# Margins in a planner that writes out the order of work: five constants of a fused attention and GLU kernel

## The chip, the cores and the metric

The kernel runs on one core of one Trainium2 chip. The metric is the device time of one execution in microseconds (us), lower is better. Before the change five runs took 881.21, 882.92, 887.68, 879.78 and 884.89 us; the median is 882.92 us. The run with 881.21 us is the one whose profile is read here.

The core has five engines, each with an instruction queue of its own that it works off in order: TensorE (PE, matrix products into PSUM), ScalarE (ACT, here exp), VectorE (DVE), GpSimd (POOL) and SyncE (SP, which here issues all transfers). An instruction that waits holds up everything behind it on its engine.

## The reference

The input has 2048 rows of width 640, all in bf16. One block of attention (32 heads of width 20) and one of a bilinear GLU (width 1728) follow each other, each on a normalised copy of its input:

```python
qkv = (x @ wqkv).reshape(B, S, 3, H, Dh) ...
scores = jnp.einsum("bhqd,bhkd->bhqk", q, k) * (Dh ** -0.5)
p = _softmax(scores, axis=-1)
o = jnp.einsum("bhqk,bhkd->bhqd", p, v)
...
h = x + _A_ref(_layernorm(x, axis=-1), A_wqkv, A_wo)
h2 = h + _B_ref(_layernorm(h, axis=-1), B_w_gate, B_w_up, B_w_down)
```

`_B_ref` is `((x @ w_gate) * (x @ w_up)) @ w_down`. The exp of the scores is the largest piece outside the products: 32 heads of 2048 by 2048.

## The kernel before

**Tiling.** The queries are cut into five chunks (`CHUNKS`, L37: three of 512 columns, two of 256), the heads into eight groups of four. A unit of attention is one PSUM bank: scores of 128 keys against 512 queries of one head (or two key tiles against 256 queries), transposed, so that keys lie on partitions. There are 2048 units. Four heads run side by side in the rows of TensorE for the scores (L1008), and side by side in its columns for the product with V (L1159), which adds up in the one bank ACC. V carries a column of ones, so that the sums of the softmax come out of the same product.

**Two ways for exp.** ACT takes three banks at once (SA into a buffer EA) or two (SB into EB), L1083. DVE takes a unit from one of the banks D0 and D1: L1108 turns a score into the bits of a bf16 exponential with one multiply and add, into a buffer Y. L1118 makes two shifted copies of it, and L1116 a third on POOL; the sum of the four is the approximation of exp. TensorE adds them up, so a unit of DVE brings four products with V where a unit of ACT brings one.

**Background jobs.** Everything else on TensorE is a list of jobs: the projections to Q, K and V, the output projection (WO), and for each half of a chunk (256 rows) the gate and up products (14 jobs) and the down products (4 jobs). A job takes a bank (D0 or D1 while attention runs, any bank after it), issues its products (L1334 in the column mode, L1311 over the full array) and is read by DVE: L329 copies, L842 multiplies gate by up into HH, L766 and L869 add the residual. When the last group of a half has its softmax sums, a layer normalisation follows (L433 to L458, and a transposing transfer L<-t, L474), then the gate and up jobs.

**The order is planned in Python.** The kernel does not loop over tiles. A list scheduler runs while the kernel is built: it has a clock `now[0]`, gives each operation a length by a formula (`c_act`, `c_psum`, `c_fast`, `c_pool`, L67 to L80), lets each engine take the ready operation with the lowest key, and writes instructions down in the order in which its clock starts them. Only the order is kept. On the chip, semaphores make every instruction wait for what it needs, in that order. If the plan expects a result too early, the instruction stands at the head of its queue and blocks the others; if it expects it too late, other work goes first.

**What the plan expects of results.**
- `LAT` (L60, 0.12): from the end of an operation on ACT, DVE or POOL to its reader on another engine.
- `LATP` (L61, 0.23): from the end of a product, as planned (0.216 for 512 columns), to its reader. It is used where a job's bank is read (`job_done`, L1280), where ACT reads a set (L1085), where DVE reads a D bank (L1094), where a buffer that a product has read comes free (L1161) and where ACC is read (L1176).
- `dma` (L352): a transfer takes `dur` on SP's queue and lands `lat` later, 1.25 unless stated.

**The end of a group** (`close_group`, L1173). When a group of heads has all its products, DVE copies ACC to `acs` (L1188). A transfer puts the row of sums into HBM (`dscr<-acs`, d1), a second fetches it spread over the partitions (`dn<-dscr`, d2, L1191), DVE takes the reciprocals (`rn`, L1192, with the most urgent key of DVE, -2), a third transfer writes them back, a fourth broadcasts them (`bc<-rscr`), POOL multiplies (L1217), and further transfers put the result into ON for the output projection. There are 40 such groups.

**What TensorE does next** (`pe_turn`, L1410). First, if a set SA or SB is free and the next unit's Q and K are there (`stream_ready`, L978), it refills that set (`refill`, L1032); with it go those D banks that `d_banks` (L1508) grants, whose units DVE then takes (`take_for_dve`). So a unit goes to DVE only if a D bank is free at the moment of a refill. Otherwise up to four rounds are filled with background jobs whose inputs are there (`job_ready`, L1231) and with products with V whose exp is there (`counts`, L1340). [...]

Of the kernel before, what the change touches and what calls it, by code (L numbers as in the profile page):

```python
# [57 lines left out]


LAT = 0.12  # L60
LATP = 0.23  # L61
DMA_LAT = 1.5
SWITCH = 0.105
WINDOW = 3.413
# [2 lines left out]
def c_act(n):  # L67
    return 0.10 + 0.833e-3 * n


def c_psum(n):
    return 0.075 + 1.04e-3 * n
# [73 lines left out]
def kernel(  # L146
# [21 lines left out]
    dscr = [dram.tile([1, 2048], F32, name=f"dscr{i}") for i in range(NDS)]  # L168
# [18 lines left out]
    DN = [sb.tile([P, 16], F32, name=f"dn{i}") for i in range(NDS)]  # L187
# [40 lines left out]
    now = [0.0]  # L228
    lockt = {"DVE": 0.0, "POOL": 0.0}

    def tick(t):
        heapq.heappush(wake, t)
# [7 lines left out]
    def finish(op, t, e=None, end=None):  # L240

        op.done = t
        for u in op.users:
            u.left -= 1
            u.avail = max(u.avail, end if e is not None and isinstance(u, Op) and u.engs == (e,) and e != "SP" else t)
            if u.left == 0:
                if isinstance(u, Op):
                    enqueue(u)
                else:
                    release_later(u.avail, u.cb)  # L250
        op.users = []
        tick(t)

    def add(engs, dur, fn, key, deps=(), **kw):
        if isinstance(engs, str):
            engs = (engs,)
        op = Op(engs, dur, fn, flat(key), deps, **kw)
        if op.left == 0:
            op.avail = max(op.avail, now[0])
            enqueue(op)  # L260
        return op
# [3 lines left out]
    def release_later(t, f):  # L265
        seq[0] += 1
        heapq.heappush(later, (t, seq[0], f))
        tick(t)

    def after(deps, cb):  # L270
        c = Call()
        c.left = 0
        c.avail = now[0]
        c.cb = cb
        for d in deps:
            if d.done is None:
                d.users.append(c)
                c.left += 1
            else:
                c.avail = max(c.avail, d.done)  # L280
        if c.left == 0:
            release_later(c.avail, cb)
# [48 lines left out]
    attn = {"started": False, "over": False}  # L331
# [20 lines left out]
    def dma(o, i, key, deps=(), dur=0.6, lat=1.25, kb=0):  # L352

        def hook(t, end, e):
            landed[0] = max(landed[0], end + 0.3) + kb / 330.0
            op.lat = max(lat, landed[0] - end + 1.1)
        op = add("SP", dur, lambda e: nc.sync.dma_start(o, i), key, deps, lat=lat, hook=hook)
        return op

    with tc.manual_schedule():  # L360
# [325 lines left out]
        for ci in range(len(CHUNKS)):  # L686
            q0, cw = CHUNKS[ci]
            b, off = q0 // 512, q0 % 512
# [289 lines left out]
        def stream_ready(i):  # L978
            if i >= len(stream):
                return False  # L980
            ci, g, j, kts = stream[i]
            t = now[0] + 1e-9
            for m in qj[ci, g]:
                if m.done is None or m.done > t:
                    return False
            for kt in kts:
                for m in kj[g, kt // 4]:
                    if m.done is None or m.done > t:
                        return False
            return True  # L990
# [41 lines left out]
        def refill(name, dbanks):  # L1032
# [51 lines left out]
            z = Mark()  # L1084
            z.done = end + LATP  # L1085
            act_q[name] = c_act(512 * n)
            add("ACT", c_act(512 * n), fn, (1,), [z], hook=hook, gate=lambda: bool(st["efree"]))

        def fill_d(i, it, end):
            bank = banks["D"][i]  # L1090
            bank_use["D"][i] = "exp"
            z = Mark()
            z.done = end + LATP
            ys = [None] * 4  # L1094
# [54 lines left out]
        def emit_piece(j):  # L1149
# [10 lines left out]
                             start=(n == 0), stop=last, tile_position=(0, 32 * j), skip_group_check=True)  # L1160
            release_later(end + LATP, rel)  # L1161
            if last:
# [10 lines left out]
        def close_group(ci, g, end):  # L1173
            q0, cw = CHUNKS[ci]
            z = Mark()
            z.done = end + LATP  # L1176
            k = ngrp[0] % 2
            d = ngrp[0] % NDS
            ngrp[0] += 1
            a = ACS[k]  # L1180
            acc_ready[0] = 1e9
            cg_i[0] += 1

            def hook(t, en, e):
                acc_ready[0] = en + LAT
                tick(en + LAT)
            deps = [z] + ([acs_use[k]] if acs_use[k] is not None else [])
            ev = add("DVE", c_psum(cw), lambda e: nc.vector.tensor_copy(a[:, 0:cw], ACC[:, 0:cw]), (-2,), deps, hook=hook)  # L1188
            n = cw // 32
            d1 = dma(dscr[d][0, 0:4 * cw].rearrange("(a q) -> a q", a=4), a[Dh:P:32, 0:cw], 10, [ev] + ([ds_use[d]] if ds_use[d] is not None else []), kb=8)  # L1190
            d2 = dma(DN[d][:, 0:n], dscr[d][0, 0:4 * cw].rearrange("(b c) -> b c", c=n), 10, [d1], dur=0.33, kb=8)  # L1191
            rc = add("DVE", 0.07 + 0.0064 * n, lambda e: nc.vector.reciprocal(RN[d][:, 0:n], DN[d][:, 0:n]), (-2,), [d2])  # L1192
            d3 = dma(rscr[d][0, 0:4 * cw].rearrange("(b c) -> b c", c=n), RN[d][:, 0:n], 10, [rc], dur=0.33, kb=8)
            ds_use[d] = d3
            bdeps = [d3] + ([bc_use[0]] if bc_use[0] is not None else [])
            src = rscr[d][0:1, 0:4 * cw]
            bsrc = bass.AP(tensor=src.tensor, offset=src.offset, ap=[[cw, 4], [0, 32], [1, cw]])
            d4 = [dma(BC[0][:, 0:cw], bsrc, 10, bdeps, lat=1.8 + cw / 200.0)]

            parts = []  # L1200
            for j in range(4):
                f = 20 * (4 * g + j)
                m = min(Dh, P - f % P)
                parts.append((32 * j, f, m))
                if m < Dh:
                    parts.append((32 * j + m, f + m, Dh - m))
            need = [c for c in range(KT) if any(f // P == c for _, f, _ in parts)]

            def room():
                return sum((ci, c) not in on_of for c in need) <= len(on_free) and lt_ops[NT - 1].done is not None  # L1210

            def mhook(t, en, e):
                for c in need:
                    if (ci, c) not in on_of:
                        on_of[ci, c] = on_free.pop(0)
            o = OS[k]
            mu = add("POOL", 0.1 + 2.3e-3 * cw, lambda e: nc.gpsimd.tensor_tensor(  # L1217
                o[:, 0:cw], a[:, 0:cw], BC[0][:, 0:cw], ALU.mult), (0,), d4 + os_use[k], lock=True, hook=mhook, gate=room)

            def out_of(p0, f, m):  # L1220
                return add("SP", 0.75, lambda e: nc.sync.dma_start(ON[f % P:f % P + m, on_of[ci, f // P], 0:cw], o[p0:p0 + m, 0:cw]),
                           (10,), [mu], lat=DMA_LAT)
            os_use[k] = [out_of(*p_) for p_ in parts]
            after(os_use[k], lambda: finish(mu_mark[ci, g], now[0]))
            acs_use[k] = mu
            bc_use[0] = mu
# [4 lines left out]
        def job_ready(jb):  # L1231
            if jb.can is not None and not jb.can():
                return False
            if jb.target > spos[0] + SLACK and attn["started"] and not attn["over"] and recent(now[0]) > BUSY:
                return False
            for d in jb.deps:
                if d.done is None or d.done > now[0] + 1e-9:
                    return False
            return True

# [36 lines left out]
        def job_done(jb):  # L1277
            cur_job[0] = None
            z = Mark()
            z.done = jb.end + LATP  # L1280
            op = jb.evac(banks[jb.bank[0]][jb.bank[1]], z)
# [58 lines left out]
        def counts():  # L1340
            if cg_i[0] >= len(order_cg) or acc_ready[0] > now[0] + 1e-9:
                return None
            ci, g = order_cg[cg_i[0]]
            out_ = []
            for j in range(4):
                n = 0
                for pc in pieces_q.get((ci, g, j), ()):
                    if pc[2] > now[0] + 1e-9:
                        break
                    m = vj[g // 2, pc[0]].out  # L1350
                    if m.done is None or m.done > now[0] + 1e-9:
                        break
                    n += 1
                out_.append(n)
            return out_
# [68 lines left out]
            return keep_busy()  # L1424

        BUSY = 0.55
        SLACK = 1000

        def keep_busy():

            t = now[0]
            if t < T0 or spos[0] >= len(stream) and not jq and cur_job[0] is None:
                return False
            if recent(t) > (BUSY if attn["started"] else BUSY0):
                tick(t + 0.25)
# [20 lines left out]
        ROUND = 0.216  # L1456
        SCORE = 0.216 + LATP
        MARGIN = 0.05
# [46 lines left out]
        def bg_wanted():  # L1505
            return cur_job[0] is not None or any(job_ready(jq[k]) for k in range(min(LOOK, len(jq))))
# [99 lines left out]
```

The softmax here doesn't subtract the row's maximum and nothing guards it: scores larger than these inputs give would overflow.

## Time and profile before

| | value |
|---|---|
| median of five runs | 882.92 us |
| the profiled execution, by its run's time | 881.21 us |
| its span, first to last instruction | 879.4 us |
| mean granted clock of TensorE | 0.986 |
| ACT, instructions on exp (EA, EB) | 323 and 319 |
| DVE, units of exp (L1108) | 445 |
| POOL, busy | 332.9 us (38%) |

The span falls into three parts: some 24 us of loads, normalisation and first projections, the attention from 24 us to 815 us, with background jobs in between, and 64 us after it in which the last two halves of the GLU are done. The profile's lists name an engine and a line; `EA<-SA` is an instruction that writes tile EA from SA. "Idle before" is the time an engine stood still ahead of an instruction, with the engine whose result ended the wait. Dividing groups into instructions: 323 instructions of three banks and 319 of two make about 1603 units on ACT, with some of fewer banks among them, and 445 are left for DVE.

### The profile page before, as it was taken

The page shows a single profiled execution, that of the slowest core. Times are in us where ns is not written, and L with a number is a line of the kernel's source. Part 1 is how long each engine was busy: PE and PEld are TensorE (multiplying, and loading weights), DVE is VectorE, ACT ScalarE, POOL GpSimd, SP SyncE. Part 2 cuts the span into 40 slices and gives each one's busy share as a digit, 9 for nine tenths or more (in the row PEclk, how much of TensorE's full clock was granted, in tenths as well). Part 3 has the DMA queues.
Part 4 walks back from the last instruction along what each step waited for, and adds up shares of the span by engine and source line. Part 5 has one row for each costly group of instructions (what it writes and reads, how often), then busy time and mean ns, then how long its engine had stood idle before and what let it go on. Part 6 is the DMA issues. An engine that isn't in the chain of part 4 may idle for free.

```text
span 879.4 us, 36714 instructions
## 1 busy us (share of the span) xinstructions
PE 822.9 (94%) x15755; PEld 413.3 (47%) x15755; DVE 725.3 (82%) x1938; ACT 770.7 (88%) x718; POOL 332.9 (38%) x498
## 2 busy tenths in 40 slices
PE   5999899899998999999998999999999999999988
PEld 4433434333333444444334444444455555555866
DVE  4888888788898998888998898998989888789343
ACT  3899999899998999999999999999999999999211
POOL 1023444344443434344554444444544333444100
PEclk8999999899999999999999999999999999999999
DMA  8274321212246301010111021010111111002100
GB/s 271 42 176 126 102 71 35 93 54 75 62 120 136 79 26 54 23 48 24 31 29 36 22 37 38 19 45 29 32 34 35 39 40 35 19 17 48 32 17 16
DMA packets 70547, 49.80 MB, mean 57 GB/s; under 512 B 33712, under 2 KB 66448, under 8 KB 70384
## 3 DMA queue, kind: packets, MB, share of 16 engines
q1 hardware_dynamic: 70384, 47.46, 20.0%
q8 instruction: 123, 2.02, 1.0%
q14 instruction: 40, 0.33, 0.1%
HBM read 30.88 MB, written 10.32 MB: 47 GB/s over the span
## 4 chain that ended last, share of the span: by engine, by line
PE 54%; DVE 22%; ACT 9%; DMA 8%; issue 5%; SPq 2%; POOL 1%; DVEq 0%; POOLq 0%; ACTq 0%
PE D L1334 19%; PE ACC L1159 14%; DVE Y L1108 7%; PE SA L1008 6%; PE D L1311 5%; DVE Y L1118 5%; PE SB L1008 5%; ACT EA L1083 5%; ACT EB L1083 4%; DMA dn<-dscr 3%; PE D L1008 3%; DVE HH L842 2%; DVE lst L433 2%; DMA dscr<-acs 2%; DVE gs L329 1%
## 5 line engine op out<-in xcount | busy, mean ns | idle before, releaser
L1083 ACT ACTIVATE EA<-SA 128x1536 bf16<-128x1536 f32 x323 | 468.5, 1450 | 21.5 <-PE SA L1008 16.7
L1116 POOL TENSOR_SCALAR Y<-Y 128x512 uint16<-128x512 uint16 x445 | 284.9, 640 | 446.1 <-DVE Y L1118 290.0
L1108 DVE TENSOR_SCALAR Y<-D 128x512 uint16<-128x512 f32 x445 | 303.2, 684 | 59.2 <-PE D L1008 18.8
L1083 ACT ACTIVATE EB<-SB 128x1024 bf16<-128x1024 f32 x319 | 328.4, 1029 | 17.7 <-PE SB L1008 11.1
L1159 PE MATMUL ACC<-Y,VX 128*32 128x512 bf16 (+1 forms) x2244 | 264.9, 341 | 4.3 <-DVE acs L1188 3.5
L1118 DVE TENSOR_SCALAR Y<-Y 128x512 uint16<-128x512 uint16 x890 | 239.3, 312 | 8.7
L1159 PE MATMUL ACC<-EA,VX 128*32 128x512 bf16 (+1 forms) x1203 | 210.5, 343 | 1.2 <-ACT EA L1083 0.9
L1159 PE MATMUL ACC<-EB,VX 128*32 128x512 bf16 (+1 forms) x796 | 179.1, 343 | 0.0
L1334 PEld LDWEIGHTS <-R 128*32 128x32 bf16 x5370 | 129.4, 96 | 99.4 <-issue 78.8
L1008 PE MATMUL D<-QT,KTt 20*128 20x512 bf16 (+1 forms) x561 | 169.6, 339 | 6.8 <-DVE Y L1108 3.4
L1159 PEld LDWEIGHTS <-VX 128*32 128x32 bf16 x4243 | 122.5, 97 | 94.5 <-issue 72.8
L1008 PEld LDWEIGHTS <-KTt 20*128 20x128 bf16 x2560 | 71.9, 91 | 197.3 <-issue 187.0
L1334 PE MATMUL D<-L,R 128*32 128x256 bf16 x3240 | 136.6, 275 | 11.0 <-DVE HH L842 7.6
L1008 PE MATMUL SA<-QT,KTt 20*128 20x512 bf16 (+1 forms) x1203 | 129.3, 342 | 4.6 <-ACT EA L1083 3.2
L1008 PE MATMUL SB<-QT,KTt 20*128 20x512 bf16 (+1 forms) x796 | 126.5, 342 | 1.0 <-ACT EB L1083 0.2
L1334 PE MATMUL D<-R 128*32 128x160 bf16 (+1 forms) x2090 | 105.3, 300 | 4.7 <-DVE VX L329 3.2
L1334 PE MATMUL D<-R,HH 128*32 128x320 bf16 x1236 | 63.4, 301 | 2.2 <-DVE HH L842 2.2
L1217 POOL TENSOR_TENSOR os<-acs,bc 128x512 bf16<-128x512 f32 (+1 forms) x40 | 43.3, 1081 | 49.9 <-DMA bc<-rscr 35.3
L842 DVE TENSOR_TENSOR HH<-D,gs 128x256 bf16<-128x256 f32 x104 | 43.9, 423 | 18.6 <-ACT gs L327 15.8
L1334 PEld LDWEIGHTS <-HH 128*32 128x32 bf16 x1236 | 33.0, 96 | 22.8 <-issue 18.1
L329 DVE CAST gs<-D 128x256 bf16<-128x256 f32 x84 | 34.6, 412 | 1.6 <-PE D L1334 1.1
L1334 PE MATMUL D<-WO,ON 128*32 128x320 bf16 x560 | 31.2, 302 | 3.6 <-DVE hr L766 2.5
(72 smaller groups left out, 389.9 us busy)
## 6 DMA issues: line engine op xcount, KB each, us to landing
bc<-rscr SPq DMA_DIRECT2D x24, 256.0 KB
KTt<-kscr SPq DMA_DIRECT2D x6, 512.0 KB
QT<-qscr SPq DMA_DIRECT2D x22, 128.0 KB
t<-in_A_x_dram SPq DMA_DIRECT2D x16, 160.0 KB
out_dram<-t SPq DMA_DIRECT2D x16, 160.0 KB
bc<-rscr SPq DMA_DIRECT2D x16, 128.0 KB
R<-in_B_w_gate_dram SPq DMA_DIRECT2D x4, 480.0 KB
R<-in_B_w_up_dram SPq DMA_DIRECT2D x4, 480.0 KB
```

The lines of the kernel that those rows point to most:

```text
L329: nc.vector.tensor_copy(o, i)
L433: halves_ = [add("DVE", 0.41, lambda e, i=i, c=c: nc.vector.bn_stats(st[:, i, c, :], tiles[i][:, c * 320:(c + 1) * 320]), (key, i), deps) ...
L842: mu = add("DVE", c_psum(256), lambda e: nc.vector.tensor_tensor(HH[0:M, f, :], bank[0:M, 256:512], GS[k][0:M, :], ALU.mult), EVK, mdeps)
L1008: nc.tensor.matmul(bank[:, n * cw:(n + 1) * cw], lhsT=KTt[32 * j:32 * j + Dh, g, kt * P:(kt + 1) * P], rhs=QTt[32 * j:32 * j + Dh, g, 0:cw ...
L1083: nc.scalar.activation(st["e"][eslot["i"]][:, 0:n * 512], src[:, 0:n * 512], ACT.Exp, scale=SCALE)
L1108: p_ = add("DVE", c_psum(512), lambda e: nc.vector.tensor_scalar(YT[ys[0]][:, :], bank, scalar1=EXP_A, scalar2=EXP_B, op0=ALU.mult, op1=AL ...
L1116: nc.gpsimd.tensor_scalar(o, i_, scalar1=float(d), scalar2=1.0, op0=ALU.add, op1=ALU.mult)
L1118: nc.vector.tensor_scalar(o, i_, scalar1=float(d), scalar2=None, op0=ALU.add)
L1159: nc.tensor.matmul(ACC[32 * j:32 * j + 32, 0:cw], lhsT=VX[:, kt, h * VS:h * VS + 32], rhs=ap, start=(n == 0), stop=last, tile_position=(0, ...
L1217: mu = add("POOL", 0.1 + 2.3e-3 * cw, lambda e: nc.gpsimd.tensor_tensor(o[:, 0:cw], a[:, 0:cw], BC[0][:, 0:cw], ALU.mult), (0,), d4 + os_u ...
L1311: nc.tensor.matmul(bank[0:M, c0:c1], lhsT=lhs(0, M), rhs=rhs(), start=first, stop=last, skip_group_check=True)
L1334: nc.tensor.matmul(bank[32 * j:32 * j + 32, c0:c1], lhsT=lhs(32 * j, 32 * j + 32), rhs=rhs(), start=first, stop=last, tile_position=(0, 32 ...
```

## The change

Five constants of the planner change. `LATP` falls from 0.23 to 0.12. The plan adds a margin `GQ` of 0.5 to the landing of Q and K before a unit may be issued (once attention has begun), `GJ` of 1.0 to everything that a background job reads (while attention runs), and `GP` of 0.3 to each piece that a product with V reads. The landing of d2, the fetch of the softmax sums, is expected 3.0 after its issue instead of 1.25, so the reciprocal is put later into DVE's order. No instruction's form changes; their order does, and how many units go to DVE.

```diff
-LATP = 0.23
+LATP = 0.12
...
             ci, g, j, kts = stream[i]
-            t = now[0] + 1e-9
+            t = now[0] + 1e-9 - (GQ if attn["started"] else 0.0)
...
-            d2 = dma(DN[d][:, 0:n], dscr[d][0, 0:4 * cw].rearrange("(b c) -> b c", c=n), 10, [d1], dur=0.33, kb=8)
+            d2 = dma(DN[d][:, 0:n], dscr[d][0, 0:4 * cw].rearrange("(b c) -> b c", c=n), 10, [d1], dur=0.33, kb=8, lat=D2)
...
+            g = GJ if attn["started"] and not attn["over"] else 0.0
             for d in jb.deps:
-                if d.done is None or d.done > now[0] + 1e-9:
+                if d.done is None or d.done + g > now[0] + 1e-9:
                     return False
...
-                    if pc[2] > now[0] + 1e-9:
+                    if pc[2] + GP > now[0] + 1e-9:
                         break
...
         BUSY = 0.55
+        GJ, GP, GQ, D2 = 1.0, 0.3, 0.5, 3.0
```

## The prediction

> **What bounds the kernel now.** I read the busy times of two windows first, the attention (24 to 815 us) and what follows it, then the waits inside the attention, then the timeline around the longest of them.
>
> The windows (busy us of each engine, instructions in brackets, granted clock, share of DMA, GB/s):
>
> ```profile
> 24.00:815.00 791.00, 750.15 (x14723) 355.02 (x14722) 691.76 (x1849) 750.45 (x665) 327.31 (x485) 0.99 0.20 54
> 815.00:879.40 64.40, 58.69 (x613) 46.59 (x609) 22.95 (x55) 11.54 (x31) 1.80 (x3) 0.97 0.06 20
> ```
>
> In the attention TensorE and ACT are each busy for 750 of 791 us, so each stands still for about 41 us; DVE stands still for 791 - 692 = 99 us. TensorE's busy time says less, since it counts a matmul that fills a quarter of the array like a full one. ACT's says more: it has nothing but exp to do, and each unit that it doesn't take shortens it. So the length of the attention is ACT's exp plus ACT's idle time, and a gain needs less of one or the other.
>
> The waits in the attention (total us, times, longest us):
>
> ```profile
> DVE Y L1108 <- PE D L1008: 18.8, 38, 1.6
> DVE Y L1108 <- PE SA L1008: 18.5, 40, 0.8
> ACT EA L1083 <- PE SA L1008: 16.7, 31, 2.2
> DVE Y L1108 <- PE SB L1008: 15.2, 40, 1.7
> DVE rn L1192 <- DMA dn<-dscr: 13.3, 16, 1.9
> ACT EB L1083 <- PE SB L1008: 11.1, 22, 1.2
> PE D L1334 <- DVE HH L842: 10.6, 25, 1.1
> ```
>
> ACT waits for scores that come late from TensorE (L1008). The second thing to see is the one wait for a transfer: DVE, in its fixed order, stands at the reciprocal until the sums have landed. What that does to the others is in the timeline at 165 to 169 us (start, duration, engine, instruction, idle before and its releaser):
>
> ```profile
> 167.28 0.25 DVE L1192 RECIPROCAL rn<-dn 128x16 f32<-128x16 f32 x1 [1.86 <-DMA dn<-dscr]
> 167.45 0.26 DVE L329 CAST VX<-D 128x160 bf16<-128x160 f32 x1
> ...
> 167.77 0.53 PE L1334 MATMUL D<-R 128*32 128x160 bf16 x20 [2.31 <-DVE VX L329]
> ...
> 168.45 0.39 PE L1008 MATMUL SA<-QT,KTt 20*128 20x512 bf16 x3
> ...
> 168.77 0.61 PE L1159 MATMUL ACC<-EA,VX 128*32 128x512 bf16 x1
> ...
> 168.89 1.45 ACT L1083 ACTIVATE EA<-SA 128x1536 bf16<-128x1536 f32 x1 [2.19 <-PE SA L1008]
> ```
>
> DVE stops for 1.86, the copy behind it comes late, TensorE stops for 2.31 at the bank which that copy frees, and the refill behind that reaches ACT 2.19 late. The wait passes through three engines at full size. Afterwards a matmul takes 0.61 instead of 0.38 us: the granted clock was 0.83 between 160 and 180 us, and 1.00 in most other windows of 20 us.
>
> **Part 1, d2 expected 3.0 after its issue.** The reciprocal's place in the plan moves by 3.0 - 1.25 = 1.75 us. The longest wait is 1.86, so of 13.3 us about 0.1 is left. What ACT gains is read from its timeline, as its idle time in the few us after the larger waits (reciprocal's start: ACT's idle pieces): 93.66: 1.07; 167.28: 2.19 + 0.54 + 0.30; 216.27: 0.97 + 0.49; 389.05: 0.39 + 0.25; 652.31: 0.38; 686.17: 0.49; 701.90: 0.58 + 0.36; 749.48: 1.14. The sum is 9.15 us. Ends: 0 if other lateness fills the same gaps, -13.3 if every wait counts in full. I take **-9**. Behind the reciprocal come, on SP's queue, `rscr<-rn` and `bc<-rscr`, then POOL's product and the transfers into ON; all move back by up to 1.75 us. That is covered: groups end some 20 us apart (40 in 791 us), and POOL is busy for 327 of 791 us. At the last group the cover is the other half's GLU; without it, 1.75 us.
>
> **Part 2, the short way from matmul to reader.** In the plan a D bank, and a set, has its reader 0.23 - 0.12 = 0.11 sooner, and a unit goes to DVE only if a D bank is free at a refill. There are 323 + 319 = 642 refills in 791 us, one each 1.23 us, and 445 units went to DVE, 0.69 for each refill. 0.11 is 9% of 1.23; if the banks alone decided, DVE would take 9% more, 40 units. Ends: 0, and what DVE's 99 idle us hold. A unit costs DVE 1.0 us (0.60 from a L1108 to the next instruction, 0.20 for each of two L1118, at 384 to 386 us), so at most 99. I take 24, nearer to 40 than to 99 because background jobs hold the second bank and DVE does not always have its time where a bank is free. ACT starts at 499.42 (three banks), 500.75 (two) and 501.65, that is 0.44 to 0.45 us for each bank. So 24 units are 24 x 0.45 = **-11** (ends 0 and -45). TensorE pays three products more for each, 3 x 0.216 / 4 = 0.16, in all +3.9, and saves 24 / 2.5 = 10 refills with two changes between row and column mode, whose idle weight-load time is 187.0 us in 607 pieces, 0.31 each: -6. I count that as 0.
>
> **Part 3, the price of the short way.** The real way is longer. At 382 us DVE was idle and waiting:
>
> ```profile
> 382.10 0.39 PE L1008 MATMUL SB<-QT,KTt 20*128 20x512 bf16 x1
> ...
> 382.55 0.69 DVE L1108 TENSOR_SCALAR Y<-D 128x512 uint16<-128x512 f32 x1 [0.32 <-PE SB L1008]
> ```
>
> From matmul start to reader are 0.45 us; the plan before had 0.216 + 0.23 = 0.45, the plan after has 0.34. The old value was right; the new one is 0.11 short. DVE waited for scores at 118 of 445 units; each such wait can grow by 0.11. It reaches the path where TensorE then waits for a bank: 25 (HH) and 6 (Y) times now, and I let the number double: 62 x 0.11 = 7, of which part falls where ACT has its next set filled. I take **+5**. Ends: -2 (DVE stands ready sooner) and 469 units x 0.11 = +52, if each is passed on.
>
> [...]
>
> **Part 4, margins GJ, GP, GQ.** They let TensorE do other work when a result is only just due. What they can remove are its waits for inputs: in the attention L1334 behind VX 3.2, L<-t 1.7, L1118 1.3 and L 0.6, L1159 behind EA 0.9 and Y 0.6, L1008 behind QT 0.9 and KTt 0.9; in all 10.1 us, of which 2.3 of VX is already in part 1. The wait on L<-t (1.7, at 276.7 us) cost ACT 1.69 + 0.78 + 0.64 = 3.1; a margin of 1.0 takes some 1.8 of that. Waits for a bank (HH 10.6) aren't touched: a bank is no input. Gain: -3, end -8. Price: 1.0 at each step of a half's chain (WO, normalisation, gate and up, down), 4 x 8 halves = 32 us if the chain decided all along; it is hidden by other jobs, as the list usually has some that are ready, and if that cover is gone for a tenth of it, +3. GP delays the end of a group by 0.3, 40 x 0.3 = 12 at the worst, while TensorE has background work and ACT runs on into free buffers. I take +2 for both. GQ delays only units whose K or Q has just landed, a few in the first 60 us. Net **-1**, ends -8 and +12.
>
> **Part 5, what is late next.** A shorter attention leaves less time for background work beside it. That streams some 219 us in 791 (gate and up 3240 x 0.109 / 4 = 88, down 1236 x 0.14 / 4 = 43, WO 20, projections 68), 0.28 us in each. With 16 us gone, up to 4.5 move into the part after attention; TensorE's own idle 41 us takes some. I count **+3**, ends 0 and +10.
>
> **Sum:** -9 - 11 + 5 - 1 + 3 = -13 on a span of 879.4: 866.4. The profiled run was 881.21, 1.8 over its span, and 1.7 under the median of 882.92; with both the forecast is **870 us**, 13 less than the median.
>
> **Rivals.**
>
> *DVE becomes the bound (slower).* Its mechanism is part 3 alone: DVE takes units that it can't start when the plan says, TensorE reaches a D bank that isn't free yet, and ACT's refill stands behind it. For it: DVE is the engine that TensorE waits for most, and the old value matched the trace. Against it: 99 us of idle time on DVE. It decides from about 180 late units on, where 180 x 0.11 = 20 us eat parts 1 and 2. With 300 of 469 passed on (33 us) and no push into the tail, -9 - 11 + 33 - 1 = +12: 895 us.
>
> *The short way changes nothing in the count.* DVE stays near 445 units, since the second bank is held by jobs or DVE's own backlog decides. Then part 2 is 0, and part 5 about 1: -9 + 5 - 1 + 1 = -4, 879 us. For it: a unit also needs four free Y buffers and DVE's time.
>
> *DVE takes many.* 60 units, -27, with lateness +8 and tail +6: -9 - 27 + 8 - 1 + 6 = -23, 860 us. For it: DVE's 99 idle us hold them; against it: DVE would be busy for over 94% of the attention.
>
> **How the numbers follow.** The forecast (860 to 877) gets 0.47, many units 0.14, an unchanged count 0.17, DVE as the bound 0.22. A measurement of this kernel tells about 0.5% from no change, so faster means under 878.5, slower over 887.3. Faster: 0.47 + 0.14 + 0.05 of the unchanged count = 0.66; same: the other 0.12 of it and 0.01 of the slow case = 0.13; slower 0.21. The range takes in the slow case up to 893 and the quick one down to 852, with some 0.2 outside.
>
> **What would show it.** Right: reciprocal waits on `dn` under 2 us in all; about 470 L1108; ACT's idle in the attention near 30 us; waits of DVE on L1008 above 52.5 us; the attention 16 us shorter, the part after it about 3 longer. Wrong: the same count of L1108 (part 2); TensorE's waits for DVE's readers above 30 us (part 3); a tail above 70 us (parts 4 and 5).

## The result and the profile after

The changed kernel takes 880.14 us (median of 53 runs, 874.24 to 884.12), the kernel before 882.72 us beside it (95 runs). The ratio is 0.9999, 95% interval 0.9985 to 1.0013: no change, where 870 us and 13 us less were forecast. Ratios in this document compare fast runs alone, without those over 1.5% above the fastest of their kernel, which leaves out 32 of these 95 runs of before, none of the 53, and 18 of the 35 runs of before beside the first four runs of the table below. The quotient of the two medians is 0.997. A second comparison, among the experiments below, gave 0.9938 (0.9899 to 0.9977). So the change is worth between nothing and 1%.

The profiled execution of the changed kernel took 883.89 us with a span of 882.1 us and a granted clock of 0.978. Most of its runs are shorter: over the 53 runs the median clock is 0.986, and time and clock go together (correlation -0.72). It is read for what it shows of waits, not for its length.

For both kernels I cut the windows at the first and the last exp of ACT, before first, then after (busy us of PE, PEld, DVE, ACT, POOL; clock; DMA share; GB/s):

```profile
25.50:814.30 788.80, 747.96 (x14689) 353.79 (x14684) 690.03 (x1844) 749.08 (x662) 327.04 (x484) 0.99 0.21 54
814.30:879.40 65.10, 59.39 (x629) 47.23 (x622) 23.22 (x57) 11.54 (x31) 2.08 (x3) 0.97 0.06 20
```

```profile
24.30:812.10 787.80, 753.31 (x14605) 351.78 (x14607) 710.56 (x1899) 739.33 (x652) 339.91 (x502) 0.98 0.20 53
812.10:882.10 70.00, 63.82 (x665) 49.42 (x658) 26.53 (x65) 11.57 (x32) 4.74 (x7) 0.97 0.09 25
```

ACT has 9.8 us less to do, close to the 11 that were forecast, and DVE 20.5 us more; 466 units go to DVE instead of 445. But the attention is only 1.0 us shorter. ACT's idle time grew from 39.7 to 48.5 us: what it no longer computes it waits. TensorE's idle time fell from 40.8 to 34.5 us. The part after the attention grew from 65.1 to 70.0 us.

The waits in the attention of the changed kernel, answering to those shown of before (in its file the lines behind L1231 stand one or two lower, so L1335 answers to L1334; the waits of POOL and of weight loads are left out):

```profile
DVE Y L1108 <- PE SB L1008: 19.0, 43, 1.9
ACT EA L1083 <- PE SA L1008: 16.4, 28, 3.1
ACT EB L1083 <- PE SB L1008: 15.3, 35, 1.3
DVE Y L1108 <- PE SA L1008: 14.4, 29, 4.0
DVE Y L1108 <- PE D L1008: 12.9, 30, 1.1
...
PE ACC L1159 <- DVE acs L1188: 6.7, 15, 1.6
PE D L1008 <- DVE Y L1108: 6.3, 11, 1.4
...
PE D L1008 <- DMA QT<-qscr: 3.1, 1, 3.1
...
PE D L1335 <- DVE HH L842: 1.6, 5, 0.4
DVE rn L1192 <- DMA dn<-dscr: 1.5, 3, 0.6
```

Three lines of before that its list ahead of the result doesn't show:

```profile
PE ACC L1159 <- DVE acs L1188: 3.5, 8, 1.2
PE D L1008 <- DVE Y L1108: 3.4, 6, 1.6
...
PE D L1008 <- DMA QT<-qscr: 0.9, 1, 0.9
```

The wait for d2 is nearly gone (13.3 to 1.5), and so is most of TensorE's wait behind HH (10.6 to 1.6). A stall of 3.1 us on a transfer of Q has come (0.9 before), and TensorE waits longer for banks that DVE hasn't read yet: ACC 3.5 to 6.7, Y 3.4 to 6.3.

By an estimate from the clock, the stall on Q cost more than its length. The windows of 20 us in which the changed kernel's clock fell (before it fell to 0.83, 0.95, 0.97 and 0.91 in four):

```profile
80.00:100.00 20.00, 17.32 (x222) 5.20 (x225) 11.87 (x31) 12.90 (x12) 6.31 (x9) 0.74 0.35 114
180.00:200.00 20.00, 18.93 (x255) 6.78 (x254) 16.29 (x44) 16.32 (x15) 7.59 (x13) 0.83 0.19 50
...
260.00:280.00 20.00, 18.96 (x298) 7.49 (x297) 17.77 (x51) 17.00 (x17) 7.63 (x11) 0.92 0.42 116
580.00:600.00 20.00, 18.70 (x328) 8.50 (x324) 17.53 (x46) 16.89 (x15) 9.15 (x13) 0.91 0.07 21
640.00:660.00 20.00, 17.94 (x392) 10.20 (x389) 16.96 (x48) 17.27 (x16) 10.66 (x16) 0.91 0.11 28
```

At the first of them the timeline has the stall and what follows:

```profile
79.07 0.39 PE L1335 MATMUL D<-R 128*32 128x512 bf16 x4
...
82.53 0.58 PE L1008 MATMUL D<-QT,KTt 20*128 20x512 bf16 x1 [3.07 <-DMA QT<-qscr]
...
83.20 1.45 ACT L1083 ACTIVATE EA<-SA 128x1536 bf16<-128x1536 f32 x1 [3.14 <-PE SA L1008]
```

TensorE waits 3.07 us, and the matmul behind it takes 0.58 instead of 0.38. Adding (1 - clock) x 20 over all windows from 60 us to the end of the attention gives some 14 us lost after and 6.8 before. In this execution, then, 6 us less idle time and 7 us more lost to the clock cancel, and the longer last part remains. Over its runs the changed kernel has a median clock of 0.986, and the kernel before has 0.985 or 0.986 on each chip of the experiments, so the clock explains this execution and not the medians. That in the medians the 6 us of idle time are set off by the 5 us of a longer last part is a reading of these two traces, not shown by a run.

### The profile page after: what moved, and what is told of

It reads as the page before. It is cut to its first block, busy times and chain, and to the rows that moved or that the text cites. A ratio compares the mean times of both kernels' runs of the same rounds, so it can differ in the third digit from the quotient of the medians.

```text
span 882.1 us, 36718 instructions
## 1 busy us (share of the span) xinstructions
PE 834.5 (95%) x15715; PEld 415.0 (47%) x15715; DVE 750.1 (85%) x2002; ACT 761.0 (86%) x709; POOL 348.4 (40%) x519
## 4 chain that ended last, share of the span: by engine, by line
PE 63%; DVE 27%; issue 4%; DMA 3%; ACT 2%; POOL 0%; SPq 0%; DVEq 0%; POOLq 0%; ACTq 0%
PE D L1335 22%; PE ACC L1159 16%; DVE Y L1108 10%; DVE Y L1118 8%; PE SA L1008 7%; PE D L1312 6%; PE SB L1008 5%; PE D L1008 5%; DVE lst L433 2%; DVE gs L329 1%; DVE HH L842 1%; PE ACC L1449 1%; DVE acs L1188 1%; ACT EA L1083 1%; ACT EB L1083 1%
## 5 line engine op out<-in xcount | busy, mean ns | idle before, releaser
L1083 ACT ACTIVATE EA<-SA 128x1536 bf16<-128x1536 f32 (+1 forms) x319 | 462.8, 1451 | 30.2 <-PE SA L1008 16.4
L1116 POOL TENSOR_SCALAR Y<-Y 128x512 uint16<-128x512 uint16 x466 | 301.0, 646 | 417.8 <-DVE Y L1118 260.8
L1108 DVE TENSOR_SCALAR Y<-D 128x512 uint16<-128x512 f32 x466 | 317.6, 684 | 53.2 <-PE SB L1008 19.0
L1159 PE MATMUL ACC<-Y,VX 128*32 128x512 bf16 (+1 forms) x2348 | 270.1, 341 | 7.9 <-DVE acs L1188 6.7
L1118 DVE TENSOR_SCALAR Y<-Y 128x512 uint16<-128x512 uint16 x932 | 254.4, 319 | 6.9
L1159 PE MATMUL ACC<-EA,VX 128*32 128x512 bf16 (+1 forms) x1188 | 217.5, 345 | 0.0
L1008 PE MATMUL D<-QT,KTt 20*128 20x512 bf16 (+1 forms) x587 | 177.3, 340 | 11.0 <-DVE Y L1108 6.3
L1335 PEld LDWEIGHTS <-R 128*32 128x32 bf16 x5370 | 126.3, 96 | 94.0 <-issue 76.4
L1335 PE MATMUL D<-L,R 128*32 128x256 bf16 x3240 | 129.2, 274 | 2.8 <-DVE HH L842 1.6
L1335 PE MATMUL D<-R 128*32 128x160 bf16 (+1 forms) x2130 | 111.4, 308 | 4.3 <-DVE L L329 1.7
L1335 PE MATMUL D<-R,HH 128*32 128x320 bf16 x1176 | 62.4, 303 | 0.0
L1335 PEld LDWEIGHTS <-HH 128*32 128x32 bf16 x1176 | 30.6, 96 | 22.2 <-issue 15.9
L327 ACT CAST gs<-D 128x256 bf16<-128x256 f32 (+1 forms) x28 | 10.4, 373 | 33.7 <-PE D L1312 21.9
```

The source lines that it names most:

```text
L1008: nc.tensor.matmul(bank[:, n * cw:(n + 1) * cw], lhsT=KTt[32 * j:32 * j + Dh, g, kt * P:(kt + 1) * P], rhs=QTt[32 * j:32 * j + Dh, g, 0:cw ...
L1083: nc.scalar.activation(st["e"][eslot["i"]][:, 0:n * 512], src[:, 0:n * 512], ACT.Exp, scale=SCALE)
L1108: p_ = add("DVE", c_psum(512), lambda e: nc.vector.tensor_scalar(YT[ys[0]][:, :], bank, scalar1=EXP_A, scalar2=EXP_B, op0=ALU.mult, op1=AL ...
L1116: nc.gpsimd.tensor_scalar(o, i_, scalar1=float(d), scalar2=1.0, op0=ALU.add, op1=ALU.mult)
L1118: nc.vector.tensor_scalar(o, i_, scalar1=float(d), scalar2=None, op0=ALU.add)
L1159: nc.tensor.matmul(ACC[32 * j:32 * j + 32, 0:cw], lhsT=VX[:, kt, h * VS:h * VS + 32], rhs=ap, start=(n == 0), stop=last, tile_position=(0, ...
```

## The experiments

The relief runs and rn_const keep the order of work of before. A relief run makes one engine's instructions shorter by leaving out part of the work, so its output isn't the reference's; rn_const takes a wait away in the same manner. The other runs change the planner. Each ran beside the kernel before on the same chip; the table holds five chips, so ratios are compared and not times.

| run | what | ratio to before (95%) |
|---|---|---|
| rn_const | no wait for d2 | 0.9932 (0.9897 to 0.9966) |
| relief_act | ACT, each exp 96 columns shorter | 1.0064 (0.9999 to 1.0128) |
| relief_pe | TensorE, a quarter of DVE's products | 0.9916 (0.9873 to 0.9960) |
| relief_dve | DVE some 60 us less | 0.9966 (0.9916 to 1.0016) |
| relief_rows | TensorE's scores a quarter narrower | 0.9926 (0.9885 to 0.9967) |
| relief_rows_dve | the last two together | 0.9859 (0.9803 to 0.9915) |
| relief_three | these two and relief_act | 0.9883 (0.9836 to 0.9931) |
| relief_rows_dve_rn | relief_rows_dve, and no wait for d2 | 0.9605 (0.9560 to 0.9651) |
| d2_only | D2 | 0.9866 (0.9834 to 0.9898) |
| latp_only | LATP 0.12 | 0.9979 (0.9950 to 1.0008) |
| margins_only | GJ, GP, GQ | 0.9978 (0.9945 to 1.0011) |
| latp_22 | LATP 0.22, meant as a mere reshuffle | 0.9934 (0.9898 to 0.9969) |
| no_latp | D2, margins | 0.9940 (0.9900 to 0.9980) |
| d2_latp | D2, LATP | 0.9888 (0.9837 to 0.9938) |
| d2_latp_gj | D2, LATP, GJ | 0.9863 (0.9826 to 0.9900) |
| after_again | all of it | 0.9938 (0.9899 to 0.9977) |
| after_wd | all, down weights later | 0.9913 (0.9880 to 0.9946) |
| d2_latp_q0 | D2, LATP, Q first | 0.9898 (0.9856 to 0.9939) |

**What bounds the attention.** Theory A is the prediction's (ACT's exp plus its idle time). The rivals are B, TensorE's own stream of matmuls, and C, DVE behind the plan.

```diff
+        nc.vector.memset(CN[:], 2048.0)
...
-            rc = add("DVE", 0.07 + 0.0064 * n, lambda e: nc.vector.reciprocal(RN[d][:, 0:n], DN[d][:, 0:n]), (-2,), [d2])
+            rc = add("DVE", 0.07 + 0.0064 * n, lambda e: nc.vector.reciprocal(RN[d][:, 0:n], CN[:, 0:n]), (-2,), [d2])
```

> The kernel before, instruction for instruction, but the reciprocals read a constant tile instead of the landed sums (the softmax is not normalised), so DVE never waits for d2 there. Theory A (the prediction's: the attention is ACT's exp plus ACT's idle time, and the waits for d2 make 9 us of that idle time): about 9 us faster, 871 to 876 us, and ACT idle near 31 us in the attention. Theory B (TensorE's own stream sets the pace of the attention; a stall of DVE is made up for elsewhere in the same order): less than 4 us faster.

0.9932, 6 us (3 to 9). Order and instructions are those of before, so this is the wait's own worth: two thirds of the 9 us of part 1, which lies at the end of the interval, and more than theory B expected. The medians of all runs, 871.38 against 883.48 us, are 12 us apart; 6 is the lower of the two readings.

```diff
-                nc.scalar.activation(st["e"][eslot["i"]][:, 0:n * 512], src[:, 0:n * 512], ACT.Exp, scale=SCALE)
+                nc.scalar.activation(st["e"][eslot["i"]][:, 0:n * 512 - 96], src[:, 0:n * 512 - 96], ACT.Exp, scale=SCALE)
```

> The order of before, with each exp of ACT 96 columns shorter (the last 96 columns of each set are left out): 642 instructions x 96 columns x 0.82 ns = 51 us of ACT's work less. Theory A: 35 to 51 us faster. Theory B (TensorE is the bound of the attention): under 12 us faster, ACT's idle time grows by the rest.

Not faster at all: 1.0064. (Fills of the buffers on POOL stand at the start, ahead of its first other work; the attention starts at 24.0 us, not later than before.) The instructions are 55 us shorter in sum (1450 to 1365 ns and 1029 to 943 ns on average). In the window from 24 to 815 us ACT was busy for 711.4 instead of 750.5 us:

```profile
24.00:815.00 791.00, 747.57 (x14641) 351.33 (x14633) 689.69 (x1839) 711.42 (x661) 325.73 (x483) 0.99 0.21 54
```

Its waits for TensorE rose (the lines of this run's file stand two lower):

```profile
ACT EA L1085 <- PE SA L1010: 31.9, 85, 1.5
ACT EB L1085 <- PE SB L1010: 26.1, 54, 1.7
```

Before they were 16.7 and 11.1. ACT's idle time in this window rose by the same 39 us: it only waits longer for the same fills. Theory A falls.

```diff
-            kt, ap, t, rel = pieces_q[key].popleft()
+            kt, ap, t, rel, skip = pieces_q[key].popleft()
...
-            nc.tensor.matmul(ACC[32 * j:32 * j + 32, 0:cw], lhsT=VX[:, kt, h * VS:h * VS + 32], rhs=ap,
+            if not skip or n == 0 or last:
+              nc.tensor.matmul(ACC[32 * j:32 * j + 32, 0:cw], lhsT=VX[:, kt, h * VS:h * VS + 32], rhs=ap,
```

Here `skip` marks one of the four products of a unit of DVE.

> The order of before without one of the four products with V of each unit of DVE (the sum lacks that quarter): 445 x 0.216 / 4 = 24 us less of TensorE's stream, ACT and DVE as before. Theory A: under 5 us faster. Theory B: 15 to 24 us faster, ACT idle under 25 us.

0.9916, 7 us of 24. In its trace TensorE's own time (the attention less TensorE's idle time less half of the time at half clock) is 736.9 us against 741.0 before, so only 4 us of the 24 left TensorE's stream, and no time in the attention ran at half clock, against 13.7 us before. Why so little of the stream goes isn't shown; the four products of a round start within 0.01 us of each other and the next round 0.22 us later (at 386.95 us, before), so one of them less need not end the round sooner. So this settles little.

```diff
-                        nc.vector.tensor_scalar(o, i_, scalar1=float(d), scalar2=None, op0=ALU.add)
+                        nc.vector.tensor_scalar(YT[ys[dst]][:, 0:256], YT[ys[src_]][:, 0:256], scalar1=float(d), scalar2=None, op0=ALU.add)
```

> The order of before with the two shifted copies of DVE (L1118) half as wide (256 of 512 columns are left out): 890 instructions of 0.2 us become some 0.13, about 60 us less of DVE's work. Theory A and B: under 8 us faster. Theory C (DVE is late against the plan, TensorE stands at banks that DVE has not read): 15 us or more faster, and TensorE's waits for DVE's readers fall to near nothing.

0.9966, not clear of 1 (the medians of all runs are 7 us apart, 876.34 and 883.48). Theory C alone, which expected 15 us or more, falls too: DVE was busy for 637.9 instead of 691.8 us in the window from 24 to 815 us, and little or nothing came of it.

```diff
-                    nc.tensor.matmul(bank[:, n * cw:(n + 1) * cw],
+                    nc.tensor.matmul(bank[:, n * cw:(n + 1) * cw - cw // 4],
...
-                                     rhs=QTt[32 * j:32 * j + Dh, g, 0:cw], start=True, stop=True, skip_group_check=True)
+                                     rhs=QTt[32 * j:32 * j + Dh, g, 0:cw - cw // 4], start=True, stop=True, skip_group_check=True)
```

> The order of before with the score products (L1008) a quarter narrower (384 of 512 columns, 192 of 256; the rest of each bank keeps what was in it; four fills of banks with zeros are added at the start). A refill is a stretch of its own on TensorE, between two changes of mode, so 642 refills x 128 columns / 2.4 GHz = 34 us of TensorE's stream go, and nothing of ACT's or DVE's work. Theory B (attention = some 740 us of TensorE's own stream + its idle time + the loss at half clock): 20 to 34 us faster. If the time is set by the in-order waits between all engines and not by TensorE: under 10 us faster.

0.9926, 6 or 7 us where B expected 20 to 34. B in its plain form falls as well. TensorE's own time did fall, from 741.0 to 712.1 us, by 29 of the estimated 34 (642 x 128 columns x 0.42 ns: in the trace of before, four products side by side follow the four ahead of them after 216 ns with 512 columns and 109 ns with 256, medians). Where these 29 us went is in the waits of the whole span (lines two lower than before), with the one of before behind them:

```profile
DVE rn L1194 <- DMA dn<-dscr: 23.1, 22, 2.1
PE D L1336 <- DVE HH L844: 17.2, 28, 2.4
...
PE D L1010 <- DVE Y L1110: 7.7, 17, 1.6
```

```profile
DVE rn L1192 <- DMA dn<-dscr: 13.9, 17, 1.9
```

The wait for d2 grew from 13.9 to 23.1 us, and TensorE waits behind DVE. With TensorE faster, DVE reaches the reciprocal earlier (4.95 instead of 5.10 us after its copy of ACC, median), and the transfers take as long as before: from the issue of d1 to that of d2 the median is 1.76 us in both traces, and where DVE waited, the reciprocal started 2.8 us (before) and 2.7 us after the issue of d2. TensorE's idle time in the attention rose from 40.8 to 62.5 us, and the median clock of its runs fell to 0.979.

> Two reliefs at once in the order of before: score products a quarter narrower (34 us of TensorE, alone -0.7%) and DVE's shifted copies half as wide (about 60 us of DVE, alone -0.3%). If TensorE and DVE bound the attention together, each taking over where the other is relieved: 20 us or more faster, TensorE's waits for DVE's readers back under 20 us. If a third thing holds it (ACT, transfers, the clock): about the sum of the two single runs, 9 us.

0.9859, 12 us of the some 94 taken out: between the two expectations, some 3 us beyond the sum of the single runs, whose intervals cover that, so that no interplay of the two is shown. The wait for d2 stayed at 22.6 us.

> The two reliefs and ACT's (96 columns less in each exp, 51 us of ACT's work, alone +0.6%). If ACT is the third that takes over: 15 us or more beyond the run with two reliefs. If ACT plays no part: within 5 us of it. If the clock takes it, the time at half clock in the attention is above 35 us.

0.9883. The fills on POOL made the attention start at 33.8 instead of 26.9 us, so the lengths of the attention are compared: 776.5 us, and 775.2 with two reliefs. ACT is not the third. The wait for d2 was 28.0 us in the attention.

> The run with two reliefs (score products a quarter narrower, shifted copies half as wide; 0.986 of before), and the reciprocals read a constant, so that DVE doesn't wait for d2 (22.6 us of waits in the run with two reliefs). If the waits for transfers are what takes over when the engines are relieved: 8 us or more beyond the two reliefs, 864 us or less, and TensorE idle under 45 us. If the clock takes it: within 4 us of the two reliefs, with 25 us or more at half clock in the attention.

0.9605, 849.59 us. Taking the wait for d2 out of the run with two reliefs is worth 22 us (872.08 to 849.59, on two chips whose kernels before differ by 1.5 us), though the same step in the order of before was worth 6, or 12 by the medians. TensorE was idle for 41 us in the attention, and 10 us of it ran at half clock, against 53 and 27 us in the run with the wait. The attention ends at 782.4 us here and at 802.1 with the wait, so the window from 24 to 815 us, first with the wait and then without, also holds 13 and 33 us of the last part:

```profile
24.00:815.00 791.00, 737.87 (x14851) 368.97 (x14841) 643.20 (x1862) 742.27 (x674) 320.34 (x486) 0.98 0.21 54
```

```profile
24.00:815.00 791.00, 749.63 (x15105) 382.41 (x15100) 648.74 (x1881) 742.89 (x683) 319.03 (x487) 0.99 0.21 55
```

What follows: no single engine bounds the attention. TensorE's stream and the landing of d2 hold each other in one fixed order: each relief alone gives little, and together with the wait's removal they give 35 us. The way of d2 took the same time with faster engines (1.76 us from the issue of d1 to that of d2, median, in the relief runs too), so it takes over. ACT is not among them. Whether DVE's work is, is not shown: no run has narrower scores and no wait for d2 with DVE's work as before.

**Where D2's gain goes.**

> The late landing of d2 alone (3.0); LATP 0.23, no other margin; 449 units on DVE. Prediction's part 1: -9 us, about 872. Theory B (TensorE's stream is the bound): within 3 us of before.

0.9866, 12 us; 7.2 us of waits for d2 are left. The wait as a whole was worth 6 us (3 to 9) in rn_const, and half of it is still there, so much of the 12 is probably the other order that comes with the edit. That is argued and not shown: by the medians the wait is worth 12.

> LATP 0.12 alone; 463 units on DVE instead of 445. Prediction's parts 2 and 3 scaled to 18 units: -8 + 5 = -3 us. Lateness as the bound: 5 to 20 us slower, with TensorE's waits for DVE up from 17 us. Theory B: within 3 us.

> GJ, GP and GQ alone; 454 units on DVE. Prediction's part 4: -1 us (ends -8 and +12). If the margins are what ate up the gain: 5 us slower or more, with a longer part after the attention.

0.9979 and 0.9978. Neither step alone does anything that can be told from nothing. LATP alone puts 463 units on DVE; its interval holds 0 and also the -3 us that parts 2 and 3 give for 18 units, so this run doesn't decide about their price.

> A change without meaning: LATP 0.22 instead of 0.23, so that the order is shuffled; 456 units on DVE. It shows how far time moves by a reshuffle alone. If such scatter is small, under 2 us; if single edits of the plan can't be told from it, 4 us or more either way.

0.9934 (0.9898 to 0.9969) for a reshuffle without meaning. So an edit of this planner can move time by 0.7% by its order alone, and single comparisons within a per cent don't name an edit.

> The change without its first line: D2 and the three margins, LATP 0.23; 455 units on DVE. If LATP 0.12 ate up the gain of D2: 870 to 875 us, as D2 alone. If the margins did: 878 us or more. A reshuffle alone moved a run by 0.7%, so a step under 6 us tells neither.

> D2 and LATP 0.12, no margins. If LATP ate up the gain: 878 us or more; if the margins did: 870 to 875 us.

0.9940 and 0.9888: without the margins, D2 keeps its gain beside LATP; with the margins and LATP 0.23 half of it is gone. That speaks against LATP as what ate it up, but the step of 0.5% is no larger than a reshuffle.

> The changed kernel, once more beside the kernel before on the chip of the other experiments. By the first comparison: within 0.2% of before, that is 880 to 886 us here. If it belongs with D2 alone and D2 with LATP (0.987 and 0.989 of before): 873 to 876 us, and the margins cost nothing.

0.9938, beside 0.9866 and 0.9888 for D2 alone and D2 with LATP on other chips: the changed kernel probably doesn't belong with them, though the intervals touch.

> D2, LATP 0.12 and of the margins GJ alone. If GJ is what puts down products behind the attention (12 jobs there instead of 11) and gives D2's gain back: a part after the attention of 68 to 70 us instead of 65, and 878 to 882 us. If GJ costs nothing: 873 to 877 us.

0.9863: GJ doesn't cost the gain, and my guess falls. The last part is longer, 68.7 us as expected, with 12 down jobs behind the attention instead of the 10 of before, but the attention is shorter by more. GJ isn't needed for that: d2_only, without it, has a last part of 68.0 us. In the part after the attention, before and then here:

```profile
L1311 PE MATMUL D<-R,HH 128*128 128x320 bf16 x140 | 19.7, 299 | 0.0
```

```profile
L1312 PE MATMUL D<-R,HH 128*128 128x320 bf16 x168 | 23.9, 299 | 0.0
```

From here to the changed kernel only GP and GQ are added, and the time goes from 0.9863 to 0.9938. Whether one of them costs it, or the order that happens to come out, was not told apart; a reshuffle is as large. Seen together, none of the ten planner runs of the table is above 1, and the four fastest are those with D2 and without GP and GQ (0.986 to 0.990): a sign that D2 is worth about 1%, from few orders.

**The stall near 80 us.** D2, LATP and the change itself share it.

```diff
-        wq_prev[:] = lt_ops
+        wq_prev[:] = [wq_prev[0]]
```

> The changed kernel with the 10 early transfers of the down weights put behind the other GLU weights, so that they no longer run between 60 and 90 us, where qscr<-HH took 4.4 us, QT<-qscr 5.1 us, and TensorE stood still for 3.1 us and then ran 10 us at half clock. Theory B with the clock: 3.1 + 10.2 / 2 = 8 us faster than the changed kernel, 870 to 873 us, if that stall goes and no other comes. If stalls at half clock are made up for later: under 3 us.

0.9913, but the stall is still there, 3.8 us, though the fetches of the down weights stand later. The store of Q (`qscr<-HH`) took 7.3 us from issue to landing even without the weights beside it; just ahead of it on SP's queue stands the fetch of 512 KB of K. The idea fell; the gain over the changed kernel is no more than a reshuffle gives.

```diff
-            g_list(64 * g_ + KLO, 64 * g_ + KHI, [A(k_dense, i, b) for b in range(4)] + [A(q_dense0, i)])
+            g_list(64 * g_ + KLO, 64 * g_ + KHI, [A(q_dense0, i)] + [A(k_dense, i, b) for b in range(4)])
```

> D2 and LATP 0.12 without margins, and in the first chunk the Q job of a group stands before its four K jobs, so that the store of Q is no longer queued behind the fetch of 512 KB of K (the wait of 4.6 us on QT<-qscr near 80 us and the time at half clock behind it). If that stall is worth its length: 868 to 871 us. If it comes back elsewhere (K late instead of Q): 873 to 877 us.

0.9898 against 0.9888 without it. The wait of 4.6 us for Q has turned into one of 3.1 us for K (`KTt<-kscr`): it came back elsewhere.

## Why the prediction was wrong, point by point

**What bounds the kernel: wrong, and the root of the rest.** The step was "the length of the attention is ACT's exp plus ACT's idle time, and a gain needs less of one or the other". As arithmetic that is true of any engine; as a statement of cause it is not. ACT's idle time gives way. In relief_act it took up all of the 39 us by which ACT was busy for less, and in the change it grew by 9 of the 10 us that went to DVE. It was to fall to about 30 us; it was 48.5.

**Part 1, -9: mechanism right, size open.** The wait for d2 went to 1.5 us in the attention ("under 2 us in all"). That is not the later place alone: with D2 alone 7.2 us were left, and single waits in other orders reached 3.1 us (latp_22), so the longest wait of one trace was no bound. Its worth in the order of before is 6 us (3 to 9) in rn_const, or 12 by the medians, and 9 lies between them.

**Part 2, -11: the count right, the price wrong.** 466 units were counted, some 470 forecast. ACT was busy for 9.8 us less, but the attention was only 1.0 us shorter, and in relief_act 55 us less of exp in the same order gave 1.0064. So 0.45 us of ACT for each bank is no price in time; what a unit moved to DVE brings can't be told from 0. This is the step that failed: without it the sum is -2, and the result is from 0 to -6. That TensorE's side was counted as 0 fits: its own time is 741.0 us before and 739.7 after.

**Part 3, +5: not seen as a sum.** DVE's waits for scores fell (52.5 to 46.3 us), where I said they would rise. TensorE's waits for a bank did rise at two places, by 3.2 at ACC and 2.9 at Y, but those behind HH fell by 9. LATP alone gave 0.9979, so that the new value is 0.11 short of the trace's 0.45 us from matmul to reader cost nothing that could be measured; a gain and a loss that cancel are not excluded.

**Part 4, -1.** Alone it agrees (0.9978, 2 us less, with an interval that holds 0). Beside D2 the runs with GP and GQ, no_latp, after_wd and after_again, are the slower ones, but whether these two cause it stays open. The 10 us of waits that I listed were partly replaced: the one on Q is now 3.1 us, and GQ's 0.5 is far too short for it.

**Part 5, +3.** The last part grew by 4.9 us, but not for the reason given, since the attention was only 1 us shorter. In the changed kernel 154 weight loads of HH stand behind the last exp instead of 140, one down job more (14 x 0.14 = 2 us, from the 19.7 us for 140 products above), and 42 products with V of units of DVE (4.3 us busy) were still to come there, where before had 15 (1.7 us).

**Rivals.** The slow one (DVE as the bound) didn't come: with DVE relieved of 60 us the time changed by 0.3%, not clear of 0. "The short way changes nothing in the count" was wrong in its mechanism, since the count rose to 466; that its sum, -4, was nearest is luck, because it set part 2 to 0 for another reason.

**Range.** The measured 880.14 us lies inside 852 to 893; the forecast of 13 us less was too sure, at 0.66 for faster.

The fastest kernels of the study that leave nothing out are d2_latp_gj and d2_only, at 0.986 and 0.987 of before.

## What to carry to other kernels

Idle time of the engine that is busiest doesn't show that it is the bound: shorten its instructions in the same order of work, and look whether the time follows. In an order that is fixed ahead, a saved microsecond counts only if nothing else in the order, a transfer above all, is late in the same place; take two things away together before calling either harmless. Where an edit reshuffles a planned order, run a meaningless reshuffle beside it, and believe only what is larger.

## What the runs showed of the hardware

**With narrower score products TensorE's clock was lower.** With score products a quarter narrower the median granted clock over the runs was 0.979 instead of 0.986, and with DVE relieved as well 0.975. In the trace of relief_rows 30.7 us of the attention ran at half clock, before 13.7. So about 8 us went back to the clock, since half of that extra time is lost. It is not the relief as such: in relief_pe, where TensorE has fewer products, the median clock was 0.990, and with the wait for d2 taken out as well (relief_rows_dve_rn) it was 0.985 again. It went with TensorE's idle time in the attention: 62.5 us in relief_rows and 53.1 in relief_rows_dve, against 41.3 and 41.4 in these two.

**TensorE's own time hardly depended on the order.** Duration of the attention less its idle time less half of the time at half clock is 741.0 us before, 739.7 after, and 737 to 742 in all the planner's other orders; it is 705 to 712 with narrower score products. In these runs the planner's constants moved idle time and clock, not the stream.

**Half clock came in stretches of 3.4, 6.8 or 10.2 us** in the attention of both kernels (granted clock 0.50, as from 168.8 to 175.5 us before and from 82.3 to 92.5 us after). TensorE did not stand still throughout ahead of them: in the 3.4 us before each stretch, the length of the shortest, it was idle for 1.0 to 2.8 us. Nor did every pause bring one: behind pauses of 1.63 and 1.32 us (at 92.9 and 469.1 us, before) the clock stayed at 1.00. As an estimate, the wait of 3.07 us on Q cost about 3 us, and the 10.2 us at half clock behind it 10.2 / 2 = 5 us more; but a longer wait at the same place, 4.6 us in d2_latp, was followed by 6.8 us at half clock only (over 24 to 815 us the clock was 1.00 there, 0.98 in the changed kernel).
